# Value sums copied by ScalarE, a new order with banks given by distance, and row maxima turned by VectorE through memory, in a gated attention and GLU kernel

## The chip, the cores and the metric

The kernel runs on one core of a Trainium2 chip. The time is that of one execution on the device, in microseconds (us). A core has TensorE (PE in the profile, its weight loads PEld), VectorE (DVE), ScalarE (ACT), GpSimd (POOL) and the sync engine (SP), which issues nearly all DMAs here. PSUM, into which TensorE writes, has eight banks of 128 partitions by 512 floats.

## The reference

```python
# x: 1 x 2048 x 512, wqkv: 512 x 1536, wo: 512 x 512, w_gate, w_up: 512 x 1792, w_down: 1792 x 512
g = sigmoid((x * gate_w).sum(-1, keepdims=True))
q, k, v = split(x @ wqkv)                       # 32 heads of 16
p = softmax(q @ k.T / sqrt(16), axis=-1)        # for each head, 2048 x 2048
a = merge_heads(p @ v) @ wo
b = (sigmoid(x @ w_gate) * (x @ w_up)) @ w_down
out = g * a + (1 - g) * b
```

All of it is float32.

## The kernel before, in words

**Numbers.** TensorE multiplies operands in a rounded float32 form. For the projections each operand is split into a rounded part (names ending in h) and the rest (l), and a product is the sum of three products (hh, hl, lh).

**Prologue.** Under 95 us: x arrives transposed, in 16 pieces (`load_x`, L181), q and k of the first eight heads and all of v are computed, q and k go to memory (q_d, k_d) and come back head by head into the tiles qs and ks (`load_pair`, L218).

**Main loop.** Heads are taken in pairs, one in partitions 0 to 63 and one in 64 to 127 (b = 0, 1; "lanes"). TensorE's array is used in two halves, which run at once. A step is 128 keys by 1024 queries of a pair; a *half* is one of the two groups of 1024 queries of a pair (32 halves in all, 16 steps each). One turn of the loop is a *period*: two steps, 256 periods. A period k issues

- t0, t1 (`st_part`, L453): four score matmuls of 64 rows for each lane, t0 for step pair k, t1 for k + 1. The rows of qs hold q and, in rows 48, 49 (lane 0) and 112, 113 (lane 1), the row maximum of each query as a rounded part and a rest, against rows of -1 in ks; so the scores come out with the maximum taken off. ScalarE takes the exponential of each bank (L455) into p;
- m0, m1 (`sm_step`, L250): four matmuls for each lane, 20 steps and more ahead, of scores without maxima; VectorE reduces each bank to a maximum by query (L252). When a half has its 64 banks, a last reduce gives m, 128 queries by 16 columns (8 query tiles, 2 lanes; L256);
- d0, d1 (`dense`, L144): 12 half-array matmuls that fill the loop with other work: q and k of later heads, then gate and up. Each sum is made of products with the lower rows of the array (d0) and the upper (d1), which write one bank, dn. Where the side changes, at the word "turn" and at the period's end, an empty instruction of POOL (a token, L155) waits for the last matmul of the one side, and the first of the other waits for the token. ScalarE copies a finished sum out of dn (L306); gate and up go to memory (gu_d, L299), and are read back after the loop;
- `values(k)` (L468): 16 matmuls of p with v into one bank. The bank is copied (L475; by VectorE, in the first four periods by ScalarE), and POOL adds the copy to the half's sum (L485). The first copy of a half is the sum itself. A half's sum goes to memory (pv_d, L487).

**The maxima's way, before.** `put_max` runs right behind the values of the period that follows the last reduce: TensorE transposes m through an identity matrix into a bank (L262), ScalarE copies the 16 x 128 (L264), POOL splits it into the rounded part and the rest (L95, L96), and SP issues four DMAs, each from 8 partitions of 128 to a row of qs (L270).

**Order and banks.** The order of a period is a string of words, written by hand, STEADY; every matmul of scores or maxima has its bank behind a colon, a number among seven (st_65 to st_67 and sm_69 to sm_72 in the rows below; the eighth bank is dn). The values have bank 5, the transposed maxima bank 0. The last 8 periods, LAST, have no maxima left to compute and half as many dense halves. Engines work through their instructions in the order in which these are issued; a matmul into a bank waits until the bank has been read.

```python
STEADY = ("t0:2 d1 m0:4 d1 t0:1 d1 m0:3 d1 t0:6 d1 d1 turn m0:0 t0:2 t1:4 "
          "d0 m1:1 t1:5 d0 d0 m1:3 t1:6 d0 d0 m1:0 d0 t1:2 m1:4 m0:1")
SUMS, MAXIMA = 5, 0
LAST = "t0 d1 t0 d1 t0 d1 turn t0 t1 t1 d0 t1 d0 t1 d0"
```

In the first four periods "m0:0 m1:6" stands ahead of STEADY, which brings the maxima from a lead of 20 steps to one of 22. In 16 periods VectorE also computes a column of gate logits from x (`logits`, L439).

**Behind the loop** the denominators are inverted (L428), and the down projection and wo are computed and put together (L634, L638).

Of the kernel before, what the change touches and what calls it, by code (L numbers as in the profile page):

```python
# [24 lines left out]
P = 128  # L25
# [10 lines left out]
LEAD = 22  # L36
# [3 lines left out]
TAIL = 8  # L40
# [4 lines left out]
def gated_mix(ctx, tc, x, xT, wqkv, wo, w_gate, w_up, w_down, gate_w, ident, out):  # L45
# [26 lines left out]
    rec_d = dram.tile([P, 512], F32, name="rec_d")  # L72

# [5 lines left out]
    idt = keep.tile([P, P], F32, name="idt")  # L79
# [18 lines left out]
    def raw_weights(src, shape, name):  # L98
        raw = keep.tile(shape, F32, name=name + "r", tag="wr", bufs=2)
        sp.dma_start(raw, src)  # L100
        return raw, shape, name

    def raw_cols(src, c0, name):
        return raw_weights(src[:, c0:c0 + P].rearrange("(k p) f -> p k f", p=P), [P, KT, P], name)
# [72 lines left out]
    def load_x(c):  # L177
        raw = mid(f"x{c}")
        cols = slice(c * 512, (c + 1) * 512)
        for k in range(KT):  # L180
            sp.dma_start(raw[:, k, :], xT[k * P:(k + 1) * P, cols])  # L181
        return raw
# [40 lines left out]
    w_q = split_weights(raw_cols(wqkv, 0, "q0"), act, dve)  # L223
    xr = {0: load_x(0)}
    for b in range(2):
# [3 lines left out]
    w_k = split_weights(raw_cols(wqkv, D, "k0"), act, dve)  # L229
# [30 lines left out]
    def put_max(half, t):  # L260
        p, i = half
        pe.transpose(t[:16, :P], mrow.pop(half).rearrange("p a b -> p (a b)"), idt)  # L262
        raw = keep.tile([16, P], F32, name=f"mr{p}_{i}", tag="mr", bufs=2)
        act.activation(raw, t[:16, :P], AF.Copy)  # L264
        hl = keep.tile([16, 2, P], F32R, name=f"mhl{p}_{i}", tag="mhl", bufs=2)
        split(hl[:, 0, :], hl[:, 1, :], raw, pool, pool)
        for b in range(2):
            for a in range(2):
                r = 64 * b + 3 * DH + a
                sp.dma_start(QS[p % 2][r:r + 1, i * 1024:(i + 1) * 1024].bitcast(F32),  # L270
                             hl[8 * b:8 * b + 8, a, :].bitcast(F32))


    wd = []

    def filling():
        jobs = [("qk", c) for c in range(1, D // P)] + [("gu", f) for f in range(NF)] + [("down", 0)]

        def raws(kind, n):
            if kind == "qk":  # L280
                return [raw_cols(wqkv, n * P, f"q{n}"), raw_cols(wqkv, D + n * P, f"k{n}")]
            if kind == "gu":
                return [raw_cols(w_gate, n * P, f"g{n}"), raw_cols(w_up, n * P, f"u{n}")]
# [35 lines left out]
    for c in range(NC):  # L319
        if c + 1 < NC:  # L320
            split_x(c + 1, xr.pop(c + 1))
        if c == 0:
            wv_r = mid("wv_r")
            sp.dma_start(wv_r, wqkv[:, 2 * D:].rearrange("(k p) f -> p k f", p=P))
# [10 lines left out]
    sp.dma_start(idt, ident)  # L335
# [20 lines left out]
    for t in range(2, NS, 2):  # L356
        two = [Sum(bankv(), tokens(t + a)) for a in range(2)]
        for g in (LOW, UP):
            first_max()
            for m in range(3 * KT):  # L360
# [4 lines left out]
                if (0, 0) in mrow and g == UP:  # L365
                    put_max((0, 0), bankm())
# [332 lines left out]
```

## Time and profile before

| | |
|---|---|
| median of 3 runs | 1772.06 us (1772.02 to 1772.82) |
| span of the profiled execution (first to last instruction) | 1769.9 us |
| TensorE clock granted | 1.000 |
| main loop: first and last value matmuls start at | 94.9 and 1538.2 us |
| VectorE busy | 1565.4 us |
| ScalarE busy | 1209.9 us |

The profile is of one execution; 2.2 us of the median lie around its span. Rows of a timeline give the start, the duration, engine, line and operation, output <- input, shapes and a count; "[0.16 <-PE st L468]" says that the engine had been idle for 0.16 us and what ended that. Rows of groups give busy time and mean duration in ns, then idle time before them. A matmul that follows another without a wait has a duration of 0.39, one that had to wait about 0.50.

### The profile page before, as it was taken

The numbers are of one execution on the slowest core, as the hardware profiler recorded it, in microseconds if no ns is written. First come the engines' busy times: TensorE is split into PE (matmuls) and PEld (weight loads), VectorE is DVE, ScalarE is ACT, GpSimd is POOL, SyncE is SP. The second block draws the span as 40 slices with busy tenths as digits, with TensorE's granted clock in tenths as the row PEclk, the third lists the DMA queues.
The fourth block names the chain that finished last, engine by engine and source line by source line (L and its number), as shares of the span: only waits on it lengthen the run. The fifth ranks groups of instructions, "written<-read, shape, count | busy, mean of one in ns | idle before, by whom it ended". The sixth has DMA issues, their size and how long they took to land.

```text
span 1769.9 us, 33479 instructions
## 1 busy us (share of the span) xinstructions
PE 1756.4 (99%) x12708; PEld 1109.5 (63%) x12708; DVE 1565.4 (88%) x2503; ACT 1209.9 (68%) x2343; POOL 477.7 (27%) x435
## 2 busy tenths in 40 slices
PE   9999999999999999999999999999999999999999
PEld 7756566666555555555666666666565665588887
DVE  6989999999999999999999999999999997456543
ACT  4177777777777777777777777777777777844221
POOL 1124343432132222222222222222222222342110
PEclk9999999999999999999999999999999999999999
DMA  9312323241312131313031212112121212367762
GB/s 247 83 37 67 79 67 91 67 102 43 79 55 67 44 84 49 84 49 84 31 71 39 65 45 60 50 53 51 50 49 51 58 46 75 114 226 249 239 190 71
DMA packets 91633, 148.78 MB, mean 84 GB/s; under 512 B 10128, under 2 KB 37904, under 8 KB 88592
## 3 DMA queue, kind: packets, MB, share of 16 engines
q1 hardware_dynamic: 91472, 146.64, 29.9%
q8 instruction: 100, 1.64, 0.4%
q14 instruction: 61, 0.50, 0.1%
HBM read 87.10 MB, written 58.98 MB: 83 GB/s over the span
## 4 chain that ended last, share of the span: by engine, by line
PE 96%; DVE 3%; DMA 1%; issue 0%; ACT 0%; SPq 0%; DVEq 0%; POOL 0%
PE st L468 26%; PE dn L144 25%; PE sm L453 11%; PE sm L661 7%; PE sm L250 6%; PE st L250 5%; PE st L453 5%; PE st L131 4%; PE dn L661 2%; DVE stat L252 1%; PE st L144 1%; PE st L570 1%; PE sm L570 1%; PE sm L468 1%; DVE part L475 1%; DVE xn L439 1%
## 5 line engine op out<-in xcount | busy, mean ns | idle before, releaser
L252 DVE TENSOR_REDUCE stat<-sm 128x1 f32<-128x512 f32 x1554 | 971.5, 681 | 9.8 <-PE sm L250 6.3
L455 ACT ACTIVATE p<-sm 128x512 f32<-128x512 f32 x1029 | 608.5, 625 | 303.5 <-PE dn L144 196.6
L250 PE MATMUL sm<-ks,qs 48*128 48x512 f32 x1554 | 632.1, 415 | 0.1
L455 ACT ACTIVATE p<-st 128x512 f32<-128x512 f32 x1019 | 564.6, 635 | 14.3 <-PE st L453 10.7
L485 POOL TENSOR_TENSOR sum<-sum,part 128x512 f32<-128x512 f32 x224 | 289.3, 1292 | 868.9 <-PE sm L453 685.6
L468 PE MATMUL st<-p,v 128*17 128x512 f32 x4000 | 478.1, 595 | 0.0
L453 PE MATMUL st<-qs,ks 64*128 64x512 f32 x1019 | 422.8, 419 | 7.9 <-DVE stat L252 5.9
L453 PE MATMUL sm<-qs,ks 64*128 64x512 f32 x1029 | 425.2, 419 | 0.0
L252 DVE TENSOR_REDUCE stat<-st 128x1 f32<-128x512 f32 x494 | 336.5, 682 | 2.5 <-PE st L250 0.9
L453 PEld LDWEIGHTS sm<-qs,ks 64*128 64x128 f32 x1029 | 190.0, 186 | 209.5 <-issue 105.5
L250 PEld LDWEIGHTS sm<-ks,qs 48*128 48x128 f32 x1554 | 283.7, 184 | 29.4 <-DVE stat L252 10.1
L468 PEld LDWEIGHTS st<-p,v 128*17 128x17 f32 x4000 | 92.7, 96 | 216.9 <-issue 155.8
L453 PEld LDWEIGHTS st<-qs,ks 64*128 64x128 f32 x1019 | 188.6, 186 | 47.6 <-DVE stat L252 16.6
L250 PE MATMUL st<-ks,qs 48*128 48x512 f32 x494 | 195.0, 395 | 0.5 <-ACT p L455 0.5
L475 DVE COPY part<-st 128x512 f32<-128x512 f32 x216 | 149.3, 691 | 40.0 <-PE st L468 38.0
L250 PEld LDWEIGHTS st<-ks,qs 48*128 48x128 f32 x494 | 91.4, 185 | 21.2 <-ACT p L455 1.1
L417 DVE TENSOR_TENSOR gul<-gul 128x1024 f32<-128x1024 f32 (+1 forms) x30 | 46.1, 1542 | 35.9 <-ACT gul L416 33.7
L661 PE MATMUL sm<-wd_h,hl 128*128 128x512 f32 x208 | 68.3, 395 | 0.0
L306 ACT ACTIVATE gu<-dn 128x512 f32<-128x512 f32 x98 | 66.5, 679 | 0.0
L93 ACT ACTIVATE hl<-gul 128x1024 fp32r<-128x1024 f32 (+1 forms) x30 | 29.9, 997 | 40.1 <-PE sm L661 26.0
L96 POOL TENSOR_TENSOR ol<-ot,oh 128x1024 fp32r<-128x1024 f32 x8 | 19.3, 2412 | 113.8 <-ACT oh L93 113.8
L93 ACT ACTIVATE oh<-ot 128x1024 fp32r<-128x1024 f32 x8 | 8.5, 1061 | 57.0 <-DVE ot L619 51.7
(459 smaller groups left out, 2978.4 us busy)
## 6 DMA issues: line engine op xcount, KB each, us to landing
gu_d<-gu SPq DMA_DIRECT2D x112, 256.0 KB
gul<-gu_d SPq DMA_DIRECT2D x56, 512.0 KB
qs<-q_d SPq DMA_DIRECT2D x90, 128.0 KB
ks<-k_d SPq DMA_DIRECT2D x90, 128.0 KB
pv_d<-sum SPq DMA_DIRECT2D x32, 256.0 KB
q_d<-qe SPq DMA_DIRECT2D x12, 512.0 KB
k_d<-qe SPq DMA_DIRECT2D x12, 512.0 KB
x<-in_xT_dram SPq DMA_DIRECT2D x16, 256.0 KB
```

The lines of the kernel that those rows point to most:

```text
L131: pe.matmul(o, a, b, start=(i == 0), stop=(i == len(ops) - 1))
L144: mm = pe.matmul(self.o, a[rows], b[rows], start=(self.n == 0), stop=(self.n == 2 * len(self.ops) - 1))
L250: pe.matmul(t, qs[r:r + KM, qt * P:(qt + 1) * P], ks[r:r + KM, g * 512:(g + 1) * 512], start=True, stop=True)
L252: dve.tensor_reduce(stat[half][:, b, qt % 8, g:g + 1], t, axis=AX.X, op=ALU.max)
L306: leave = lambda e, o: act.activation(e, o, AF.Copy)
L417: dve.tensor_tensor(gu[:, 1, a], gu[:, 0, a], gu[:, 1, a], ALU.mult)
L453: pe.matmul(o, ks[r:r + KR, (kt + a) * P:(kt + a + 1) * P], qs[r:r + KR, q0:q0 + 512], start=True, stop=True)
L455: act.activation(pt[:, 2 * a + c, :], o, AF.Exp, scale=DH ** -0.5)
L468: pe.matmul(o[32 * c:32 * c + VW, :], v[:, 2 * k % 16 + a, h * VW:(h + 1) * VW], pts[c // 2][:, 2 * a + c % 2, :], start=(a == 0), stop=(a ...
L475: dve.tensor_copy(e, o)
L485: pool.tensor_tensor(s, s, e, ALU.add)
L661: pe.matmul(down[t], a, b, start=(f == 0 and m == 0), stop=(f == NF - 2 and m == 5))
```

## The change

1. ScalarE copies the value sum in every period.
2. The order of the period is a new string without banks. A bank is now taken by distance: the n-th allocation of the loop (t, m or values, 17 in a period) gets the bank that was given REUSE[n mod 17] allocations before.
3. The maxima are split by POOL in their [128, 16] form (`split_max`, right behind the values of the period whose last maxima they are). At the word "turn" of the next period VectorE transposes the 128 x 32 of rounded parts and rests by blocks of 32 x 32, SP stores the result in a new buffer m_d in memory (128 rows of 128 bytes), and four DMAs read from it into the rows of qs, each 32 pieces of 128 bytes (`turn_max`). TensorE's transpose, ScalarE's copy and the identity matrix are gone.
4. The lead is 20 steps throughout: the additional maxima matmuls of the first four periods are gone, and LAST begins ten periods before the end instead of eight, six of these with eight dense halves and four with six.
5. The host lays x, the weights of q and k, gate and up out by tiles of 128 x 128, so that a weight load reads 2 KB rows instead of 512 B; wv too is laid out as it is loaded. The first q and k weights are issued by ScalarE's queue, so that x comes first on SP's.

The core of the diff:

```diff
-    def put_max(half, t):
+    def split_max(half):
+        hl = keep.tile([P, 2, 16], F32R, name=f"mhl{half[0]}_{half[1]}", tag="mhl", bufs=2)
+        split(hl[:, 0, :], hl[:, 1, :], mrow.pop(half).rearrange("p a b -> p (a b)"), pool, pool)
+        turning.append((half, hl))
+
+    def turn_max():
+        half, hl = turning.pop(0)
         p, i = half
-        pe.transpose(t[:16, :P], mrow.pop(half).rearrange("p a b -> p (a b)"), idt)
-        raw = keep.tile([16, P], F32, name=f"mr{p}_{i}", tag="mr", bufs=2)
-        act.activation(raw, t[:16, :P], AF.Copy)
-        hl = keep.tile([16, 2, P], F32R, name=f"mhl{p}_{i}", tag="mhl", bufs=2)
-        split(hl[:, 0, :], hl[:, 1, :], raw, pool, pool)
+        mt = keep.tile([P, 32], F32, name=f"mt{p}_{i}", tag="mt", bufs=2)
+        dve.transpose(mt, hl.rearrange("p a b -> p (a b)").bitcast(F32))
+        sp.dma_start(m_d[p, i], mt)
+        rows = m_d[p, i].rearrange("(g a b t) j -> a b t g j", g=4, a=2, b=2)
         for b in range(2):
             for a in range(2):
                 r = 64 * b + 3 * DH + a
-                sp.dma_start(QS[p % 2][r:r + 1, i * 1024:(i + 1) * 1024].bitcast(F32),
-                             hl[8 * b:8 * b + 8, a, :].bitcast(F32))
+                sp.dma_start(QS[p % 2][r:r + 1, i * 1024:(i + 1) * 1024].bitcast(F32).rearrange(
+                    "o (t g j) -> o t g j", g=4, j=32), rows[a, b].unsqueeze(0))
...
         def put(e):
-            if k < LEAD - FIRST << 1:
-                act.activation(e, o, AF.Copy)
-            else:
-                dve.tensor_copy(e, o)
+            act.activation(e, o, AF.Copy)
...
+    given = [*seven, *seven]
+    count_given = [0]
+
+    def place():
+        b = given[-REUSE[count_given[0] % len(REUSE)]]
+        count_given[0] += 1
+        given.append(b)
+        return b
...
             if word == "turn":
                 turn(run)
                 work(1)
+                if turning:
+                    turn_max()
...
-    STEADY = ("t0:2 d1 m0:4 d1 t0:1 d1 m0:3 d1 t0:6 d1 d1 turn m0:0 t0:2 t1:4 "
-              "d0 m1:1 t1:5 d0 d0 m1:3 t1:6 d0 d0 m1:0 d0 t1:2 m1:4 m0:1")
+    STEADY = ("t0 m1 d1 m0 t0 d1 d1 m0 d1 t0 d1 m0 d1 turn t0 t1 m0 "
+              "d0 m1 m1 d0 d0 t1 d0 t1 t1 d0 d0 m1")
+    REUSE = (5, 8, 6, 6, 10, 7, 7, 6, 8, 7, 7, 6, 8, 6, 8, 7, 7)
+    LAST = ["t0 d1 t0 d1 t0 d1 d1 turn t0 t1 t1 d0 t1 d0 t1 d0 d0"] * (TAIL - 4) + [
+        "t0 d1 t0 d1 t0 d1 turn t0 t1 t1 d0 t1 d0 t1 d0"] * 4
...
-        if k < LEAD - FIRST << 1:
-            emit("m0:0 m1:6", **parts)
...
         values(k)
-        for half in ahead:
-            put_max(half, seven[MAXIMA])
+        for half in list(mrow):
+            split_max(half)
```

Three places show what this does to the queues. The first is TensorE's, in the middle of a period of the loop; L453 is t, L250 m, L144 d, L468 the values, and a wait for DVE or Activation ahead of t or m is that for its bank. Before, the second part of a period up to the values:

```order
L250 MATMUL sm_72<-ks_107,qs_106 128x512 [waits DVE_49]
L453 MATMUL st_67<-qs_106,ks_107 128x512 [waits Activation_49]
L144 MATMUL dn<-xh,g7h 128x512
L144 MATMUL dn<-xl,g7h 128x512
L250 MATMUL sm_69<-ks_107,qs_106 128x512 [waits DVE_49]
L144 MATMUL dn<-xh,g7l 128x512
L453 MATMUL sm_71<-qs_106,ks_107 128x512 [waits Activation_49]
L250 MATMUL st_65<-ks_107,qs_106 128x512 [waits Activation_49]
L250 MATMUL sm_70<-ks_107,qs_106 128x512 [waits DVE_49]
L468 MATMUL st_66<-p_1_11122,v 17x512 [waits Activation_49]
```

After (t is L460, d is L143, the values L475), from the word "turn" on:

```order
L460 MATMUL sm_69<-qs_106,ks_107 128x512 [waits DVE_49]
L460 MATMUL sm_70<-qs_106,ks_107 128x512 [waits Activation_49]
L250 MATMUL sm_72<-ks_107,qs_106 128x512 [waits DVE_49]
L143 MATMUL dn<-xh,g7h 128x512 [waits Pool_sequencer_49]
L250 MATMUL st_65<-ks_107,qs_106 128x512 [waits Activation_49]
L250 MATMUL sm_71<-ks_107,qs_106 128x512 [waits Activation_49]
L143 MATMUL dn<-xl,g7h 128x512
L143 MATMUL dn<-xh,g7l 128x512
L460 MATMUL st_66<-qs_106,ks_107 128x512 [waits DVE_49]
L143 MATMUL dn<-xh,g7h 128x512
L460 MATMUL sm_69<-qs_106,ks_107 128x512 [waits Activation_49]
L460 MATMUL st_67<-qs_106,ks_107 128x512 [waits DVE_49]
```

What moved: before, the last matmul of the period is one of maxima that waits for VectorE; after, the waits for VectorE stand at the matmul of maxima behind "turn" and at two of t1, and no maxima matmul but one is left behind them.

The second place is VectorE's queue around the end of a half of maxima (L256). Before:

```order
L252 TENSOR_REDUCE stat_0_5393<-st_65 128x1 [waits PE_49]
L252 TENSOR_REDUCE stat_0_5393<-sm_70 128x1 [waits PE_49]
L256 TENSOR_REDUCE m_0_5881<-stat_0_5393 128x16 [waits DVE_49]
L475 COPY part_5892<-st_66 128x512 [waits PE_49,Activation_49,Pool_49]
L252 TENSOR_REDUCE stat_1_5898<-st_65 128x1 [waits PE_49]
L252 TENSOR_REDUCE stat_1_5898<-sm_72 128x1 [waits PE_49]
L252 TENSOR_REDUCE stat_1_5898<-sm_69 128x1 [waits PE_49]
L252 TENSOR_REDUCE stat_1_5898<-sm_70 128x1 [waits PE_49]
```

After, with the transpose at "turn" (L269):

```order
L252 TENSOR_REDUCE stat_0_5439<-sm_70 128x1 [waits PE_49]
L252 TENSOR_REDUCE stat_0_5439<-st_66 128x1 [waits PE_49]
L256 TENSOR_REDUCE m_0_5923<-stat_0_5439 128x16 [waits DVE_49]
L252 TENSOR_REDUCE stat_1_5944<-st_67 128x1 [waits PE_49]
L252 TENSOR_REDUCE stat_1_5944<-st_65 128x1 [waits PE_49]
L252 TENSOR_REDUCE stat_1_5944<-sm_70 128x1 [waits PE_49]
L252 TENSOR_REDUCE stat_1_5944<-sm_69 128x1 [waits PE_49]
L269 STREAM_TRANSPOSE mt_0_5965<-mhl_0_5938 128x32 [waits DMAHW0_49,Pool_49]
L252 TENSOR_REDUCE stat_1_5944<-st_65 128x1 [waits PE_49]
```

What moved: the copy that stood ahead of a period's first reduce is gone, and the transpose of the maxima stands behind the fourth reduce of the period that follows their end.

The third place is SP's queue, the maxima of one half. Before, with the load of k's weights behind them:

```order
L270 DMA qs_106<-mhl_1_1347 1x8x128 [waits DMAHW4_49,Pool_49]
L270 DMA qs_106<-mhl_1_1347 1x8x128 [waits DMAHW5_49,Pool_49]
L270 DMA qs_106<-mhl_1_1347 1x8x128 [waits DMAHW6_49]
L270 DMA qs_106<-mhl_1_1347 1x8x128 [waits DMAHW7_49]
L209 DMA k_d<-qe_1_1463 128x2x512 [waits DMAHW0_49,Pool_49]
```

After:

```order
L270 DMA m_d<-mt_1_1353 128x32 [waits DMAHW4_49,DVE_49]
L275 DMA qs_106<-m_d 1x32x32 [waits DMAHW5_49,DMAHW4_49]
L275 DMA qs_106<-m_d 1x32x32 [waits DMAHW6_49]
L275 DMA qs_106<-m_d 1x32x32 [waits DMAHW7_49]
L275 DMA qs_106<-m_d 1x32x32 [waits DMAHW0_49]
L207 DMA k_d<-qe_1_1446 128x2x512 [waits DMAHW1_49,Pool_49]
```

What moved: the four transfers wait for POOL before; after, a store that waits for VectorE stands ahead of them, and the first of the four waits for that store (DMAHW4).

More of the change, by code (lines that the diff above doesn't have):

```diff
@@ L529, in gated_mix @@
         pass
-    bank = bankm = lambda: spot[0]
+    bank = bankm = place
     for k in range(NPER):
         n = 2 * k
-        if n + LEAD == NSTEP:
+        if n + FIRST == NSTEP:
             bank = bank7
```

60 lines of the change are left out of this document (30 added, 30 removed).

## The prediction

> **What bounds the kernel now.** I read the busy line of the page first, then the chain of work that ended last, then one steady period of the main loop in the timeline, engine by engine.
>
> ```profile
> PE 1756.4 (99%) x12708; PEld 1109.5 (63%) x12708; DVE 1565.4 (88%) x2503; ACT 1209.9 (68%) x2343; POOL 477.7 (27%) x435
> ...
> PE 96%; DVE 3%; DMA 1%; issue 0%; ACT 0%; SPq 0%; DVEq 0%; POOL 0%
> ```
>
> By these lines the kernel is TensorE's alone. But a busy TensorE need not be at its full rate, so I look inside a period. The rows are TensorE's: value matmuls, the first half-array matmuls behind them, the last row of maxima scores, and the next value matmuls.
>
> ```profile
> 1200.11 1.91 PE L468 MATMUL st<-p,v 128*17 128x512 f32 x16
> 1201.95 0.50 PE L453 MATMUL sm<-qs,ks 64*128 64x512 f32 x1
> ...
> 1202.29 0.39 PE L144 MATMUL dn<-xl,u9h 64*128 64x512 f32 x1
> 1202.52 0.39 PE L144 MATMUL dn<-xh,u9l 64*128 64x512 f32 x1
> ...
> 1205.32 0.50 PE L250 MATMUL sm<-ks,qs 48*128 48x512 f32 x1
> 1205.75 0.62 PE L468 MATMUL st<-p,v 128*17 128x512 f32 x4
> ```
>
> A period is 1205.75 - 1200.11 = 5.64 us. Halves in one lane follow each other every 0.23, and two lanes run at once. A period has 28 halves, so 14 slots. The first starts 1.84 behind the values and the values wait about 0.43 behind the last one's start: 1.84 + 13 x 0.233 + 0.43 = 5.30. So 0.34 of each period is waiting that "99% busy" doesn't show. VectorE in the same period:
>
> ```profile
> 1202.19 0.69 DVE L475 COPY part<-st 128x512 f32<-128x512 f32 x1 [0.16 <-PE st L468]
> 1202.79 0.68 DVE L252 TENSOR_REDUCE stat<-st 128x1 f32<-128x512 f32 x1
> 1203.39 3.07 DVE L252 TENSOR_REDUCE stat<-sm 128x1 f32<-128x512 f32 x5
> ```
>
> The reduces follow each other every (3.07 - 0.68) / 4 = 0.598. The fourth starts at 1203.39 + 2 x 0.598 = 1204.59 and ends at 1205.27. Its bank is the one that the last maxima matmul takes, and that starts at 1205.32. Here is the ring: values end (1202.02), copy (0.17 later), first reduce (0.60), fourth reduce's end (3 x 0.598 + 0.68), matmul (0.05), values (0.43), 1.91 of values: 5.64. **VectorE's copy plus four reduces set the period**, not its sum of work and not TensorE's.
>
> A second test of this: where VectorE gets more work ahead of the reduces, the period should grow by all of it. These are the starts of value matmuls around a gate-logit operation (L439), and the groups of VectorE.
>
> ```profile
> 471.64 1.91 PE L468 MATMUL st<-p,v 128*17 128x512 f32 x16
> 477.89 1.91 PE L468 MATMUL st<-p,v 128*17 128x512 f32 x16
> ```
> ```profile
> L475 DVE COPY part<-st 128x512 f32<-128x512 f32 x216 | 149.3, 691 | 40.0 <-PE st L468 38.0 <-PE dn L144 1.0 <-POOL qe L121 0.7
> ...
> L439 DVE CUSTOM_DVE_ANT_0 xn<-xn,gwb 128x512 f32<-128x512 f32 x16 | 10.9, 682 | 0.0
> ...
> L256 DVE TENSOR_REDUCE m<-stat 128x16 f32<-128x64 f32 x32 | 7.0, 220 | 1.1
> ```
>
> 6.25 instead of 5.64: 0.61 more, which is what a 0.68 operation takes of a pipelined engine. It isn't hidden at all.
>
> **The change, part by part.** *The copy and the order together.* ScalarE takes all value copies, so a reduce no longer stands behind one. In the new order a maxima matmul (m1) is in the first slot of the period. Its reduce starts about 0.53 after that slot's start (0.49 matmul, 0.04 to wake), the next ones at 1.13, 1.73, 2.33. I put the new PE order against these. The m0 behind "turn" reuses the bank of the second reduce, which ends at 1.81; with 0.05 to the weight load and 0.11 that a stalled half starts late (its row is 0.50 instead of 0.39) it starts at 1.97, where its slot is at 1.74: 0.23 lost. This hides the token between the halves of a dense sum. The last t1 reuses the fourth reduce's bank (ends 3.01, start 3.17) and is late by another 0.03. The rest is in time. Values start 3.73 behind the first slot: 3.73 + 1.84 = 5.57, or **0.07 less per period**. The ten last periods have an order of their own, so 246 x 0.07 = -17. Eight reduces are 4.8 of the 5.57, so VectorE then idles near 0.8 a period.
>
> *ScalarE as cover.* The cost of the copy there I take as nothing:
>
> ```profile
> 1202.48 1.09 ACT L455 ACTIVATE p<-sm 128x512 f32<-128x512 f32 x2 [1.08 <-PE sm L453]
> ...
> 1204.41 1.61 ACT L455 ACTIVATE p<-st 128x512 f32<-128x512 f32 x3
> ```
>
> ```profile
> 1000.00:1100.00 100.00, 100.00 (x784) 60.35 (x782) 97.39 (x162) 76.17 (x153) 25.80 (x24) 1.00 0.21 53
> 1508.00:1527.00 19.00, 19.00 (x150) 8.59 (x150) 7.38 (x7) 19.00 (x41) 4.71 (x5) 1.00 0.17 60
> ```
>
> Its operations follow each other every (1.61 - 0.66) / 2 = 0.475. The first of the two stretches, columns PE, weight loads, VectorE, ScalarE, POOL, has 153 of them in 100 / 5.64 = 17.7 periods: 8.6 each, with the 1.08 of idle time at the period's start, just when the values end. A copy fits in: 9.6 x 0.475 = 4.6 of 5.57. Were it not covered, its 0.48 would be in each period.
>
> *What VectorE's new room swallows.* The 16 logit operations: -0.61 each, -10. The 32 reductions L256 delay the ring today by up to 5.78 - 5.64 = 0.14 (the rows below), of which I take 0.10 for 31 halves: -3. The lead of 20 steps instead of 22 drops the eight extra maxima matmuls in the first four periods; 107.97 - 101.44 is 6.53, so 0.9 each: -3.6. These are the starts of values in the head, around a half of maxima, and at the two ends of the last periods.
>
> ```profile
> 101.44 1.91 PE L468 MATMUL st<-p,v 128*17 128x512 f32 x16
> 107.97 1.91 PE L468 MATMUL st<-p,v 128*17 128x512 f32 x16
> ...
> 1403.59 1.91 PE L468 MATMUL st<-p,v 128*17 128x512 f32 x16
> 1409.37 1.91 PE L468 MATMUL st<-p,v 128*17 128x512 f32 x16
> ...
> 1493.61 1.91 PE L468 MATMUL sm<-p,v 128*17 128x512 f32 x16
> ...
> 1527.42 1.99 PE L468 MATMUL sm<-p,v 128*17 128x512 f32 x16
> 1531.35 1.05 PE L468 MATMUL st<-p,v 128*17 128x512 f32 x8
> ```
>
> *The tail.* Its periods last up to 1531.35 - 1527.42 = 3.93, and the second stretch above shows ScalarE busy in all of it: eight exponentials of 0.475 make 3.8. A ninth operation makes it 4.3. Nine such periods, 38.7, replace the two longer and seven short ones between 1493.61 and 1531.35, 37.7; the dense halves in them are as many. So +1.
>
> *Layout and loads.* Weights in the loop are loaded long ahead, nothing waits for them: 0. At the front q0's load no longer stands ahead of x:
>
> ```profile
> 0.74 0.44 SPq L100 DMA_DIRECT2D q0r<-in_wqkv_dram  x1
> ...
> 3.83 0.63 ACT L93 ACTIVATE q0h<-q0r 128x512 fp32r<-128x512 f32 x1 [1.60 <-DMA q0r<-in_wqkv_dram]
> ```
>
> x is issued 0.5 sooner (one issue); at most the 1.60 of that wait goes. I take -1.
>
> These add up to -17 - 10 - 3 - 3.6 + 1 - 1 = **-34**.
>
> *The maxima's way.* Before, all is done right behind the values: PE transpose, ScalarE copy, two POOL operations, and four transfers on SP's queue.
>
> ```profile
> 1406.44 2.75 SPq L270 DMA_DIRECT2D qs<-mhl  x4
> ```
> ```profile
> L270 SPq DMA_DIRECT2D qs<-mhl x128: 634/635/1518, 78.1 to 1498.6; - x128
> ```
> ```profile
> L299 SPq DMA_DIRECT2D gu_d<-gu x112: 314/326/936, 376.9 to 1566.9; - x112
> ```
> ```profile
> PE st L453 <- DMA qs<-mhl: 0.4, 1, 0.4
> ```
>
> They are issued 0.81 into the period, 0.70 apart, and TensorE waited for one of them once in the run. Now the path is: POOL's split early in the same period; VectorE's transpose only at "turn", behind the fourth reduce; a store to memory; its landing; then four reads, which SP can issue only after it. On the clock of that period: transpose at 2.93 (fifth reduce's place), 0.2 long (no row; 0.22 is the row of L256, and it can't be under 0), store issued at 3.17. The store's landing has no row in the views. It can't be under the 0.32 of an issue; this pair, a store and the wait that it ended, gives the upper end, 1633.14 - 1629.53 = 3.61, with 128 KB behind other transfers.
>
> ```profile
> 1629.53 0.66 SPq L429 DMA_DIRECT2D rec_d<-den  x1
> ```
> ```profile
> 1633.14 1.06 ACT L93 ACTIVATE oh<-ot 128x1024 fp32r<-128x1024 f32 x1 [5.25 <-DMA rec_d<-den]
> ```
>
> I take 1.65, near the 4 KB transfers of L270, which by the trace's landing events land 1.77 behind the start of a 0.63 issue. Reads start at 4.87; each costs SP 0.32 to 0.66, I take L270's row, 0.70 apart, since they too write one row of qs from many pieces. The fourth starts at 6.97, lands at 8.74, and its matmul can start at 8.90. That period is 5.64 long (the transpose delays the fifth reduce, for which the values wait, by 0.07), so this is 3.26 in the next. There the first t1 (slot 7, due at 1.74) uses the rows: it, and everything behind it on TensorE, stands until then. Six more slots and 0.32 (the 0.43 less the 0.11 of a stalled half's start) give values at 3.26 + 1.40 + 0.32 = 4.98 instead of 3.73. **A stall of 1.25 + 0.07 = 1.32 for each of 31 halves (the first lies ahead of the loop): +41.** ScalarE and VectorE then wait for TensorE, so nothing covers it.
>
> Sum: -34 + 41 = +7 on the profiled span of 1769.9; the median of 1772.06 is 2.2 above that span, which I leave: **1779**.
>
> The Trainium skill, "DMA: Bandwidth & Descriptors", section "Anatomy of one DMA — SWDGE (gpsimd) path", speaks against this change: it gives each transfer (fitted for GpSimd's queue) a fixed 2.0 us, most of it the receipt of the write, with device memory as the heaviest target. An estimate by that page puts 2.0 for 1.65 and for 1.77, so 0.6 more per half and a time near 1797. The landing of 1.77 for the 4 KB rows is a little under its figure, and no row here shows a small store to memory.
>
> **Rivals.** *A, faster: the chain is short enough.* The one number that decides is the stall per half; it breaks even at 34 / 31 = 1.09. If SP issues the reads as fast as L299's 0.32 to 0.4, the fourth starts 1.0 sooner and the stall is about 0.35: 1772 - 34 + 11 = 1749; with the store also landing 0.4 sooner nothing is left and it is 1738. For it: most DMA rows of SP are of this length. Against it: L270 itself, and rec_d<-den with 0.66, both of few partitions. Chance 0.25.
>
> *B, slower: the period stays 5.64.* The bank distances were fitted by hand above; if ScalarE's copy, in order ahead of an exponential, frees one bank 0.07 later than the ring allows, nothing is gained in the steady periods: -34 becomes -17, 1796. For it: only 0.6 of ScalarE's idle time is left. Against: the copy falls into the 1.08. Chance 0.12.
>
> *C, slower: each hop through memory is longer.* 0.3 more in the store and in the last read (still far below the 3.61) is 0.6 per half: 1797. Chance 0.10.
>
> **How the numbers follow.** The forecast, a faster period with a stall of 1.0 to 1.7 per half, has 0.53 and by itself 1768 to 1791. The predicted time is its 1779. The range reaches into A to 1755 and over B and C to 1804; below it lies about half of A (0.12), above it 0.05. A difference under 0.2% (3.5 us) can't be told from none. Faster: A's 0.24 and 0.04 of the forecast's low end, 0.28. Same: 0.12 of the forecast and 0.01 of A, 0.13. Slower: 0.37 of the forecast, B and C, 0.59.
>
> **What would show it.** Right: values every 5.57 in periods without maxima; the first reduce behind no copy; one period per half longer by about 1.3, with TensorE's weight load of the first t1 idle on a transfer qs<-m_d; logit periods like the others. Wrong: no such wait (A); intervals of 5.6 or more without maxima and ScalarE without idle time (B); reads issued 0.7 apart but starting later than 1.7 behind the store (C). Most of all I would be wrong if the store and the four reads together take under 4.7 instead of 5.6.

## The result, and the profile after

| | before | changed |
|---|---|---|
| median | 1772.14 us (4 runs, 1772.02 to 1772.82) | 1814.53 us (4 runs, 1813.24 to 1817.0) |
| span of the profiled execution | 1769.9 | 1813.0 |
| granted clock, mean | 1.000 | 0.991 |

The ratio is 1.0242, 95% interval 1.0227 to 1.0256: 42 us slower, where 7 were forecast and the range ended at 1804. Of the four runs of the kernel with the doubled store (below), one was in a slow state of the chip (2078 us at a granted clock of 0.782); its time is left out there, and it is the one whose profile was kept.

The busy line and the chain of work that ended last, in the page of the changed kernel:

```profile
PE 1753.0 (97%) x12676; PEld 1046.7 (58%) x12676; DVE 1417.8 (78%) x2282; ACT 1341.6 (74%) x2564; POOL 467.6 (26%) x435
...
PE 84%; DMA 6%; DVE 5%; SPq 3%; issue 1%; ACT 0%; POOL 0%; POOLq 0%
```

TensorE was 96% of that chain and is 84%. DMA and SP's queue, 1% together before, are 9% of it. The starts of the value matmuls around the maxima of one half show where that is:

```profile
1016.20 1.91 PE L475 MATMUL sm<-p,v 128*17 128x512 f32 x16
1021.81 1.91 PE L475 MATMUL sm<-p,v 128*17 128x512 f32 x16
1027.45 1.91 PE L475 MATMUL st<-p,v 128*17 128x512 f32 x16
1034.29 1.91 PE L475 MATMUL st<-p,v 128*17 128x512 f32 x16
1039.91 1.91 PE L475 MATMUL sm<-p,v 128*17 128x512 f32 x16
```

Periods without maxima last 5.61 (5.64 before), the one in which the transpose stands among the reduces 5.64, the next 6.84. These are VectorE's row of that transpose, SP's rows behind it, and the row of TensorE that waited longest:

```profile
1026.63 0.20 DVE L269 STREAM_TRANSPOSE mt<-mhl 128x32 f32<-128x32 f32 x1
```
```profile
1026.86 0.32 SPq L270 DMA_DIRECT2D m_d<-mt  x1
1027.29 0.36 SPq L216 DMA_DIRECT2D qs<-q_d  x1
1028.27 2.78 SPq L275 DMA_DIRECT2D qs<-m_d  x4
```
```profile
1032.48 0.46 PE L460 MATMUL sm<-qs,ks 64*128 64x512 f32 x1 [1.28 <-DMA qs<-m_d]
```

The store is issued 0.23 behind the transpose's start, the first read 1.41 behind the store, the four reads 0.71 apart, and the matmul starts 5.85 behind the transpose's start. The wait is 1.23 by the periods' length. That is the stall that was forecast. But it isn't always so small. Here is a half of the early loop, with the same views:

```profile
127.82 0.36 SPq L207 DMA_DIRECT2D q_d<-qe  x1
129.30 0.33 SPq L270 DMA_DIRECT2D m_d<-mt  x1
132.94 2.78 SPq L275 DMA_DIRECT2D qs<-m_d  x4
```
```profile
137.07 0.76 PE L460 MATMUL sm<-qs,ks 64*128 64x512 f32 x1 [3.42 <-DMA qs<-m_d]
```
```profile
129.90 1.91 PE L475 MATMUL st<-p,v 128*17 128x512 f32 x16
140.36 3.16 PE L475 MATMUL st<-p,v 128*17 128x512 f32 x16
147.21 1.91 PE L475 MATMUL sm<-p,v 128*17 128x512 f32 x16
```

A store of 512 KB (q_d) was issued 1.5 ahead, and the small store was followed by the first read, which waits for its landing, after 3.6 instead of 1.4. The period is 10.46 long, and the one behind it 6.85 without any wait for a transfer: the matmul's duration of 0.76 and the values' 3.16 for 1.91 say why. TensorE's clock was halved. The stretches of the clock, with busy time of TensorE, weight loads, VectorE, ScalarE and POOL, then the granted clock:

```profile
132.69:136.11 3.42, 0.97 (x10) 0.48 (x6) 2.11 (x4) 1.80 (x4) 1.26 (x1) 1.00 0.03 4
136.11:142.93 6.82, 5.86 (x30) 2.83 (x30) 2.58 (x4) 2.66 (x5) 1.50 (x2) 0.50 0.00 1
279.47:282.88 3.41, 1.32 (x12) 0.78 (x8) 2.46 (x4) 2.15 (x5) 1.26 (x1) 1.00 0.03 5
282.88:289.71 6.83, 6.41 (x30) 2.83 (x30) 2.58 (x4) 2.66 (x5) 1.88 (x2) 0.50 0.35 58
...
378.45:381.87 3.42, 1.73 (x14) 1.08 (x13) 2.48 (x4) 2.56 (x5) 1.26 (x1) 1.00 0.05 8
381.87:385.28 3.41, 2.58 (x22) 1.66 (x26) 2.04 (x4) 1.91 (x4) 0.00 (x0) 1.00 0.66 117
```

A window of 3.41 us in which TensorE was busy for 0.97 or 1.32 is followed by one or two windows at 0.50; one with 1.73 is not. Six waits of the loop are followed by half clock. The sum of the difference, by the starts of values in both traces (before, changed, in us):

| part | forecast | measured |
|---|---|---|
| steady periods | -17 | -6 (0.026 for 242) |
| logit periods | -10 | -10 |
| maxima reductions and the few odd periods | -3 | -4 |
| first periods (three of the four lie between two values) | -3.6 | -2.8 |
| last periods (the last half's wait among them) | +1 | +3 |
| up to the first values | -1 | +1.3 |
| waits for maxima: the usual 1.25 in 30 halves (the forecast counts 31 of 1.32) | +41 | +37.6 |
| waits for maxima: what is over 1.25 | 0 | +24 |
| sum | +7 | +43 (spans) |

### The profile page after: what moved, and what is told of

It reads as the page before. It is cut to its first block, busy times and chain, and to the rows that moved or that the text cites. A ratio compares the mean times of both kernels' runs of the same rounds, so it can differ in the third digit from the quotient of the medians.

```text
span 1813.0 us, 33225 instructions
## 1 busy us (share of the span) xinstructions
PE 1753.0 (97%) x12676; PEld 1046.7 (58%) x12676; DVE 1417.8 (78%) x2282; ACT 1341.6 (74%) x2564; POOL 467.6 (26%) x435
## 4 chain that ended last, share of the span: by engine, by line
PE 84%; DMA 6%; DVE 5%; SPq 3%; issue 1%; ACT 0%; POOL 0%; POOLq 0%
PE dn L143 14%; PE sm L475 13%; PE sm L460 11%; PE st L475 10%; PE sm L250 8%; PE st L460 8%; PE sm L670 7%; DVE stat L252 5%; PE st L250 4%; PE st L130 4%; SPq L275 3%; DMA qs<-m_d 3%; DMA m_d<-mt 3%; PE dn L670 2%; PE st L143 1%; PE sm L579 1%
## 5 line engine op out<-in xcount | busy, mean ns | idle before, releaser
L252 DVE TENSOR_REDUCE stat<-sm 128x1 f32<-128x512 f32 x1188 | 766.3, 681 | 110.0 <-PE sm L250 85.5
L462 ACT ACTIVATE p<-sm 128x512 f32<-128x512 f32 x1190 | 675.4, 622 | 35.9 <-PE st L250 26.5
L252 DVE TENSOR_REDUCE stat<-st 128x1 f32<-128x512 f32 x860 | 567.4, 680 | 119.7 <-PE st L250 101.4
L460 PE MATMUL sm<-qs,ks 64*128 64x512 f32 x1190 | 476.2, 424 | 35.1 <-DMA qs<-m_d 34.3
L250 PE MATMUL sm<-ks,qs 48*128 48x512 f32 x1188 | 475.1, 435 | 0.2
L250 PE MATMUL st<-ks,qs 48*128 48x512 f32 x860 | 364.4, 445 | 0.0
L460 PE MATMUL st<-qs,ks 64*128 64x512 f32 x858 | 342.7, 419 | 19.9 <-DMA qs<-m_d 18.0
L460 PEld LDWEIGHTS sm<-qs,ks 64*128 64x128 f32 x1190 | 221.0, 186 | 215.8 <-ACT p L462 97.0
L475 PE MATMUL sm<-p,v 128*17 128x512 f32 x2096 | 250.7, 595 | 0.0
L250 PEld LDWEIGHTS sm<-ks,qs 48*128 48x128 f32 x1188 | 214.1, 186 | 51.3 <-DVE stat L252 31.8
L475 PE MATMUL st<-p,v 128*17 128x512 f32 x2000 | 242.4, 602 | 0.0
L460 PEld LDWEIGHTS st<-qs,ks 64*128 64x128 f32 x858 | 159.0, 186 | 120.6 <-ACT p L462 49.8
L250 PEld LDWEIGHTS st<-ks,qs 48*128 48x128 f32 x860 | 155.2, 186 | 29.7 <-DVE stat L252 20.5
L479 ACT ACTIVATE part<-st 128x512 f32<-128x512 f32 x124 | 75.2, 607 | 103.8 <-issue 88.6
L475 PEld LDWEIGHTS sm<-p,v 128*17 128x17 f32 x2096 | 48.8, 97 | 122.9 <-issue 81.5
L475 PEld LDWEIGHTS st<-p,v 128*17 128x17 f32 x2000 | 46.6, 97 | 122.0 <-issue 84.4
```

Source lines behind the costliest of these rows:

```text
L250: pe.matmul(t, qs[r:r + KM, qt * P:(qt + 1) * P], ks[r:r + KM, g * 512:(g + 1) * 512], start=True, stop=True)
L252: dve.tensor_reduce(stat[half][:, b, qt % 8, g:g + 1], t, axis=AX.X, op=ALU.max)
L460: pe.matmul(o, ks[r:r + KR, (kt + a) * P:(kt + a + 1) * P], qs[r:r + KR, q0:q0 + 512], start=True, stop=True)
L462: act.activation(pt[:, 2 * a + c, :], o, AF.Exp, scale=DH ** -0.5)
L475: pe.matmul(o[32 * c:32 * c + VW, :], v[:, 2 * k % 16 + a, h * VW:(h + 1) * VW], pts[c // 2][:, 2 * a + c % 2, :], start=(a == 0), stop=(a ...
L479: act.activation(e, o, AF.Copy)
```

## Experiments

The theory is that TensorE's wait for the maxima's rows costs all of the loss, through the chain's usual lateness, late stores and the clock; the rivals are that the new order, the copies or the transfers themselves cost it.

**The order of the reads.** Lane 1's rows are needed first (t1), and are read last.

```diff
-        for b in range(2):
+        for b in (1, 0):
```

> The changed kernel (1814.5 us) with the four reads of a half's maxima issued in another order: the two for lane 1 first, which the first t1 waits for, then the two for lane 0, which are needed a period later. Theory (TensorE stands in 30 periods for the last of the four reads, 1.25 us in the usual half, and in six of them so long that the granted clock falls): lane 1's rows land 2 x 0.70 us sooner, the usual stall goes, what is left is the part by which the store landed late in the early halves (12 us in all), clock drops gone: 1814.5 - 37.5 - 11 = 1766, between 1760 and 1772. Rival (the new order with its bank distances costs the time, the waits for the reads only stand where another wait would stand anyway): within 5 us of 1814.5.

Measured: 1763.62 (1763.35 to 1763.83), ratio to before 0.9956, interval 0.9940 to 0.9973. One word in the program takes back 51 us and brings the changed kernel 8 us under the kernel before. The usual half has no wait left; the rows of the waits view are now

```profile
PE sm L460 <- DMA qs<-m_d: 5.7, 5, 1.9
PE st L460 <- DMA qs<-m_d: 3.3, 4, 1.3
```

against these of the changed kernel:

```profile
PE sm L460 <- DMA qs<-m_d: 34.3, 20, 3.4
```
```profile
PE st L460 <- DMA qs<-m_d: 18.0, 11, 2.8
```

So order, copies and layout are not what costs; the wait for these rows is.

**Transpose right behind the split.**

```diff
             split_max(half)
+            turn_max()
```

> The changed kernel with VectorE's transpose, the store and the reads issued right behind POOL's split, at the end of the period in which the last maximum is found, instead of at the word turn of the next period. Theory (only the lateness of the chain costs): it starts about 3 us sooner, which covers the usual lateness of 1.25 and the latest stores (2.2 more): all stalls in the loop go, 1814.5 - 61.5 = 1753, between 1748 and 1760. Rival (the hops through memory are themselves what costs, by contention with other transfers or by VectorE's added work): no lower than 1780.

Measured: 1775.04 (1773.07 to 1777.04), 22 over what the theory gave, under the 1780 of the rival, and 39 under the changed kernel. TensorE's waits for the rows fell from 52.3 us in 31 to 3.7 in 5, and a new wait came: VectorE stands at the transpose until POOL has split the maxima, and all reduces queue behind it. Waits view of this kernel:

```profile
DVE mt L269 <- POOL mhl L95: 28.0, 32, 2.1
```

In the usual half this makes a period 5.82 instead of 5.61; in the first six, where POOL has q and k to split first (1.9 us), 7.3 and more. The chain can be early without costing only where its input is ready.

**Work inside the wait.** Five matmuls of no use ahead of the first t1 in each period that waits; nothing of the computation changes.

```diff
+            if word == "t1" and fill_now:
+                fill_now.pop()
+                o = given[-REUSE[count_given[0] % len(REUSE)]]
+                for _ in range(5):
+                    pe.matmul(o, z.to_broadcast([P, P]), z.to_broadcast([P, 512]), start=True, stop=True)
...
+        fill_now[:] = [1] if k % 8 == 7 and k < NPER - TAIL else []
```

> The changed kernel with five matmuls of no use (128 x 512, into the bank that the next t1 overwrites) ahead of the first t1 in each period that waits for maxima, about 1.1 us of work inside the stall. Theory (an idle TensorE of some 2.9 us or more has its clock halved for 3.4 or 6.8 us, which costs 11 us over six halves of the changed kernel): the idle time stays under 2.8 in all halves, the granted clock is 1.00 in the loop and the time falls by about 11 to 1803 although work is added. Rival (the half clock falls in time that is waiting anyway, and costs nothing): 1814 or a little more, since five matmuls are added.

Measured: 1809.62 (1809.23 to 1809.91): 5 faster than the changed kernel by doing 150 matmuls more. The half-clock stretches in the loop fell from six to two, and the size was half of what I expected. All six places of the changed kernel are free of it. The two that are left (375 and 1120 us) lie behind stores that landed later in this run than in that of the changed kernel (3.7 instead of 2.6, 3.3 instead of 1.5), while the one at 746.8 (741.0 here) landed in time. So some of the 5 can be the stores' and not the clock's.

**The copies alone**, in the kernel before:

```diff
-            if k < LEAD - FIRST << 1:
-                act.activation(e, o, AF.Copy)
-            else:
-                dve.tensor_copy(e, o)
+            act.activation(e, o, AF.Copy)
```

> The kernel before (1772.1 us) with one thing changed: ScalarE copies the value sums in all periods; order, banks, lead, the maxima's way and the layout are those of before. Theory (VectorE's copy ahead of four reduces is the ring that sets the period of 5.64): the first reduce starts when the second-slot maxima matmul ends, 0.07 sooner, 17 us in all, and the logits and the reduction of maxima disappear in VectorE's idle time, 10 and 3: 1742, between 1735 and 1755. Rival (a copy in ScalarE's queue delays exponentials, and with them banks and values, by as much): within 5 us of 1772, or slower.

Measured: 1760.89 (1760.25 to 1763.53), ratio 0.9943: between the range of the theory and that of the rival. The logits' 10 us went, the period did not: 5.63 in place of 5.57. Nor did the 3 for the reduction of maxima: the period with it still lasts 5.79. Values and their weight load in this kernel:

```profile
1197.50 1.91 PE L468 MATMUL st<-p,v 128*17 128x512 f32 x16
1203.13 1.91 PE L468 MATMUL st<-p,v 128*17 128x512 f32 x16
```
```profile
1202.64 0.18 PEld L250 LDWEIGHTS st<-ks,qs 48*128 48x128 f32 x1 [0.23 <-ACT p L455]
1202.64 0.18 PEld L250 LDWEIGHTS sm<-ks,qs 48*128 48x128 f32 x1
1203.13 0.13 PEld L468 LDWEIGHTS st<-p,v 128*17 128x17 f32 x8 [0.30 <-ACT p L455]
```

TensorE now waits for an exponential, ahead of which the copy stands in ScalarE's queue, both for the last bank of maxima and for that of the values. In the median period the first reduce starts 0.07 sooner, as worked out, and the fourth ends 0.06 sooner; the period is only 0.015 shorter, so about 0.05 of it is given back between the fourth reduce and the values, where these waits for ScalarE stand.

**The old way under the new order.** PE transpose, ScalarE copy and transfers within the core, right behind the values, into the bank that the next t0 takes.

```diff
         for half in list(mrow):
-            split_max(half)
+            put_max(half, given[-REUSE[count_given[0] % len(REUSE)]])
...
```

> The changed kernel with the maxima put as before (PE transpose, ScalarE copy, POOL split, four DMAs within the core), right behind the values of the period in which the last maximum is found; order, bank distances, lead of 20, copies by ScalarE and layout stay as changed. Theory (the way through memory is what costs, order and lead are good for about 18 us together): no wait for the rows, about 0.1 more per half for the transpose and the copy, 1753 + 3 = 1756, between 1750 and 1762. Rival (a lead of 20 steps is too short for any way): the stalls stay, over 1785.

Measured: 1785.61 (1785.33 to 1786.4), what the rival gave, though not by its reason: no wait for the rows is left, but the bank was badly chosen. The transpose, the copy and the t0 stand one behind the other:

```profile
1047.53 0.27 PE L263 MATMUL sm<-idt,m 128*16 128x128 f32 x1 [0.16 <-DVE m L257]
1047.98 0.25 ACT L265 ACTIVATE mr<-sm 16x128 f32<-16x128 f32 x1
...
1048.28 0.50 PE L455 MATMUL sm<-qs,ks 64*128 64x512 f32 x1 [0.48 <-ACT mr L265]
```

That is 1.0 to 1.25 us per half of another kind (periods of 6.60 and 6.86). The time doesn't tell the theories apart; that the rows come in time at a lead of 20 steps speaks against the rival.

**A lead of 22 steps again**, everything else as changed but the last periods, of which there are eleven, with an order of their own:

```diff
-TAIL = FIRST // 2
+LEAD = 22
+TAIL = LEAD // 2
...
+        if k < LEAD - FIRST << 1:
+            bankm = lambda: given[-5]
+            emit("m0", **parts)
+            bankm = lambda: given[-6]
+            emit("m1", **parts)
+            bankm = place
...
```

> The changed kernel with a lead of 22 steps again: one more m0 and m1 in each of the first four periods, eleven last periods instead of ten; the way through memory stays. Theory (the chain misses its use by 1.25 to 3.5 us, the steps ahead decide): the maxima of a half are complete 5.6 us sooner, every stall in the loop goes; the head costs 3 or 4 more, the granted clock is 1.00 in the loop: 1814.5 - 61.5 + 4 = 1757, between 1751 and 1764. Rival (hops through memory cost by contention): over 1785.

Measured: 1756.18 (1755.66 to 1756.75), ratio 0.9908, interval 0.9893 to 0.9923: the fastest kernel of the study. No wait of TensorE for qs<-m_d is left, and the chain of a usual half is as long as in the changed kernel:

```profile
1027.38 0.32 SPq L271 DMA_DIRECT2D m_d<-mt  x1
1028.83 2.75 SPq L276 DMA_DIRECT2D qs<-m_d  x4
```

Late stores are still there: two (667.6 and 1252.3 us) landed only after 3.4 and 3.2, and TensorE didn't wait. It is not the hops but the time left for them that decides. In the first six halves there is also less to hide: the small store is now issued 4 us ahead of q_d's and not 1.5 behind it, and lands in 1.4 to 2.2.

**The store on ScalarE's queue.**

```diff
-        sp.dma_start(m_d[p, i], mt)
+        act.dma_start(m_d[p, i], mt)
```

> The changed kernel with one thing moved: the store of the turned maxima is issued on ScalarE's queue, the four reads stay on SP's. Theory (in eight halves the store landed 1 to 2.2 us late because it stood behind 512 KB and 256 KB stores in SP's queue): these halves come down to the usual 1.25, clock drops with them: 1814.5 - 12 - 11 = 1791, between 1786 and 1798. Rival (the transfers of both queues share the same engines, so the store is as late there; or ScalarE's issue costs more than it brings): within 4 us of 1814.5 or above.

Measured: 1814.42 (1812.18 to 1817.07): the rival. By the landing events of the trace the store of the same early half took 3.4 on this queue, about as late as on SP's (3.6), and those of the next five 2.3 to 2.7 (2.4 to 2.7 on SP's): another queue is no way around the large store. And the issue stands in ScalarE's queue until VectorE's transpose is done (0.23 behind its start, as on SP), with exponentials behind it:

```profile
1026.13 0.33 ACTq L270 DMA_DIRECT2D m_d<-mt  x1
1026.50 1.09 ACT L462 ACTIVATE p<-st 128x512 f32<-128x512 f32 x2 [1.33 <-PE dn L143]
```

That makes the period with the transpose 6.98 long in nearly every half (5.64 on SP's queue), and the one behind it shorter, 5.6 or some 6.3 in most (6.84 on SP's). The loss has moved; that the sum comes out as in the changed kernel is chance.

**Both: lane 1 first, and the chain behind the third reduce.**

```diff
-        for b in range(2):
+        for b in (1, 0):
...
+            elif word == "max":
+                if turning:
+                    turn_max()
...
-    STEADY = ("t0 m1 d1 m0 t0 d1 d1 m0 d1 t0 d1 m0 d1 turn t0 t1 m0 "
+    STEADY = ("t0 m1 d1 m0 t0 d1 d1 m0 max d1 t0 d1 m0 d1 turn t0 t1 m0 "
...
```

> The changed kernel with the reads for lane 1 first and with transpose, store and reads issued behind the second m0 of the period instead of at turn (VectorE's transpose then stands behind three reduces instead of four). Theory: the chain ends 1.4 + 0.6 us sooner for the first user; only a store that lands over 0.7 late can still be waited for (six early halves, two later ones, 0.3 to 1.4 each, 5 us in all), without a clock drop: 1753 + 5 = 1758, between 1752 and 1763. Rival (VectorE then waits for POOL's split, as it does when the transpose is issued right behind the split): 1768 or more.

Measured: 1762.35 (1761.77 to 1764.09), 4 over the expectation and inside its range. The early halves still wait, and the transpose now stands ahead of the reduce whose bank a t1 takes, 0.10 per half (1030.75 to 1036.46 between values, 5.71).

**What the clock costs.** The store issued twice, one behind the other (a longer chain, the same result), and the same with ten matmuls of no use inside the wait (the edit of the five above, with ten).

```diff
         sp.dma_start(m_d[p, i], mt)
+        sp.dma_start(m_d[p, i], mt)
```

> The changed kernel with the store of the turned maxima issued twice, one behind the other, so that the chain is one hop of about 1.45 us longer in each of 31 halves, and no other work is added. Theory of the clock (a window of 3.41 us in which TensorE is idle for some 1.9 us or more is followed by one at half clock, at about 1.9 us each): the idle time per half grows from 1.7 to 3.1, so four halves in five get a half-clock window: 1814.5 + 45 for the hops + 36 for the clock = 1895, and the granted clock is about 0.975. Rival (the half clock costs nothing beyond the wait): 1814.5 + 45 = 1860.

> The kernel with the store issued twice, and ten matmuls of no use (about 2.2 us) inside each wait for the maxima, so that TensorE is idle for 0.9 instead of 3.1 us per half. Theory of the clock: no half-clock windows but one or two, and the time is that of the hops alone, 1814.5 - 11 + 45 = 1848, some 45 below the same kernel without the added matmuls. Rival (the half clock costs nothing): equal to the kernel without the added matmuls, or longer.

Measured: 1921.73 (1913.45 to 1921.91) without, 1862.0 (1861.19 to 1868.86) with the added matmuls; the mean granted clock is 0.957 to 0.962 without and 0.993 to 0.996 with them. 300 matmuls more make the kernel 60 us faster. The chain is the same in both, so the half clock that the idle waits bring costs about 60 / 31 = 1.9 us more per half. That it costs time is shown, and more than the 36 that I had put; how late the stores landed without the added matmuls is not known. The kernel with the added matmuls is 14 over the 1848 that I expected for the chain alone: three half-clock stretches are left in its loop, and in 14 halves its second store landed 0.4 to 1.9 later than the usual 1.42, 12 us in all. What makes these late isn't shown.

**The additional maxima matmuls one per period**, on the kernel with the lead of 22:

```diff
-        if k < LEAD - FIRST << 1:
...
+        if k < LEAD - FIRST << 2:
+            bankm = lambda: given[-6]
+            emit(("m0", "m1")[k % 2], **parts)
```

> The kernel with the new order, the way through memory and a lead of 22 steps (1756.2 us), with the eight additional maxima matmuls one per period over eight periods instead of two per period over four. Theory (two per period make ten reduces of 0.6, over what VectorE does in a period, one per period makes nine, 5.4, which fits): the first periods cost 0.25 more each for eight of them instead of 1.27 for four: 1753, between 1751 and 1756, the fastest of all. Rival (the additional matmul waits for its bank wherever it stands): 1756 to 1762.

Measured: 1759.73 (1756.56 to 1760.88): no gain. The first periods last 6.2, which is 0.6 more than a steady one and not 0.25. In the profiled run (1760.88) one early half waits again for its rows (2.2 us), since the lead grows more slowly, and 6.83 us at half clock follow.

**The new way alone**, in the kernel before, with its lead of 22 (the edit is that of the change, part 3):

```diff
-        for half in ahead:
-            put_max(half, seven[MAXIMA])
+        for half in list(mrow):
+            split_max(half)
...
```

> The kernel before (1772.1 us) with the maxima's new way alone: POOL's split, VectorE's transpose at turn of the next period, store and four reads; order, banks, lead of 22 steps, VectorE's copies and layout as before. Theory (the way through memory takes 5.7 us or more, but costs only where less than that is left before the first use): with two more steps nothing waits; the PE transpose goes (0.1 per half), VectorE's transpose of 0.2 stands in a full VectorE (0.14 per half): 1772, between 1768 and 1777, granted clock 1.00. Rival (the way itself costs): over 1785.

Measured: 1768.78 (1767.06 to 1769.89), ratio 0.9976, interval 0.9967 to 0.9986: 4 us faster than the kernel before in the same series (1772.96). With the copies' 11 that makes 15 of the 16 by which the kernel with the lead of 22 is under before. If the parts add up, the new order with its bank distances and the layout, which come on top there, are worth about 1 together; no run has either of them alone.

## Why the prediction was wrong

**The bound now.** That VectorE's work ahead of the reduces isn't hidden held: the logit periods gave their 10 back in both kernels with ScalarE's copies. That a busy TensorE hides 0.34 of waiting in each period is worked out from rows; of this wait the change took back 0.026.

**The steady period failed by size.** 0.07 was worked out, 0.026 came. The rows of a period in the changed kernel, TensorE's first and last ones and VectorE's reduces:

```profile
1203.38 0.49 PE L460 MATMUL sm<-qs,ks 64*128 64x512 f32 x1
1203.39 0.49 PE L250 MATMUL st<-ks,qs 48*128 48x512 f32 x1
...
1206.52 0.46 PE L460 MATMUL sm<-qs,ks 64*128 64x512 f32 x1
...
1206.83 0.39 PE L143 MATMUL dn<-xh,g8l 64*128 64x512 f32 x1
1207.15 0.62 PE L475 MATMUL sm<-p,v 128*17 128x512 f32 x4
```
```profile
1203.95 0.69 DVE L252 TENSOR_REDUCE stat<-st 128x1 f32<-128x512 f32 x1 [0.73 <-PE st L250]
1204.56 2.47 DVE L252 TENSOR_REDUCE stat<-sm 128x1 f32<-128x512 f32 x4
```

The first reduce starts 0.57 behind the slot, not 0.53; the fourth ends at 3.05, not 3.01. The last t1 (its duration of 0.46 says that it waited) starts 0.09 behind that, the values 0.63 behind the t1, 3.77 behind the slot instead of 3.73. The ring is the one that I named, and the 0.044 that are missing count 242 times: 11 us. The waits view names VectorE for the values as well, whose own bank is that of the fifth reduce; but this ends 0.12 ahead of them, and where the transpose delays it by 0.12 the period grows by 0.03 only.

**The usual stall held**, in part by luck. 1.25 measured, 1.32 forecast. Transpose 0.20 as taken; the store landed in 1.40, not 1.65; the reads were 0.71 apart, taken as 0.70 (their issue has 0.65), and the last one landed in about 1.95, not 1.77. The errors of the two landings, 0.25 and 0.18, have opposite signs and nearly cancel. The Trainium skill, "DMA: Bandwidth & Descriptors", "Anatomy of one DMA — SWDGE (gpsimd) path", has a fixed 2.0 for each, fitted for GpSimd's queue. On SP's queue here the reads agree (1028.27 + 2.78 - 0.65 to 1032.48 is 2.1 with TensorE's start), the store to memory is 0.6 under it. Rival C had no part in the usual half.

**What failed is the step that took this stall as the same in all halves, with nothing behind it.** I counted 31 times one number, taken from an idle queue, and put what lies over it at nothing, without a reason; it measured 24 of the 36 us between 1779 and 1814.5 (11 more are the steady period's). Eight of the halves had a store that landed 1.0 to 2.2 later: 11 or 12 us by the landing events. Six of them are the first six, behind a 512 KB store 1.5 us ahead; I had quoted a hop of 3.61 as the upper end and put 0.10 on it, and it came here (3.6), where it had a reason that the profile of before showed (q_d and k_d are stored there). The other two (746.8 and 1351.1 us) have no such store: a 256 KB one was issued 3.5 us ahead, as in the 22 later halves that landed in 1.4 to 1.6. What the two have, and the latest of the six too, is a transfer of 16 KB of the kind that the DMA view calls "instruction" within the 1.4 us behind the issue of the store. Two late stores of the kernel with the lead of 22 (667.6 and 1252.3) have one too. That this is their cause was not tested.

**And the clock.** The clock of before is 1.00 up to the last microsecond, and its one wait for a row of maxima is 0.4 long. I let the clock stand at 1.00 under a wait that I had worked out to be over a microsecond on top of the matmul's own pipeline. What is left of the 24 us, about 12, I put down to half clock behind six waits; the pair with the doubled store gives 1.9 us per half, which fits. The six waits had 2.9 to 3.8 between the starts of two matmuls (TensorE idle for 2.5 to 3.4), and a window with TensorE busy for 1.32 of 3.41 was enough. The Trainium skill, "TensorE: Matmul & The Clock Gate", in its section "HAM oscillation — how this bites in real kernels", speaks of idle gaps over about 3.4 us. Here the clock fell sooner than that. It isn't the length of a wait alone, either: the one that ended at 382.70 was as long as another (idle for 2.5) and no half clock followed; it lay across two windows (the last two rows of the clock above).

**Front and end.** The first values came 1.3 later, not 1 sooner: a half-clock stretch lies there too (0.84 in the mean from 85 to 95 us, 1.00 before). The kernel before with the new way alone has one as well (0.85), and so has the changed kernel with the old way (0.77); the kernel with the copies alone has none. No run tested its cause. The end has periods of 4.27 with ScalarE's ninth operation, as worked out, but the first two of them last 5.10 and 5.44, the second with the last half's wait: +3.

**Rivals.** A (the chain hidden) was not what came, but it is what the smallest edit makes of the kernel: 1763.6 with two reads exchanged, inside the range for A. B's condition, an exponential late behind the copy, came true in the kernel with the copies alone, and cost there about 0.05 a period. In the changed kernel its first sign came as well, intervals of 5.6 and more (5.61), but not the second: ScalarE is idle for 1.0 in each period. C's condition, reads later than 1.7 behind the store, was met in the eight late halves, where it cost more than C's 0.6.

## What to carry to other kernels

A chain that misses its use by a microsecond is cheapest mended by what the first user needs first: the order of four reads was worth 51 us here, and two steps of lead 58. Work out a new wait for the busiest stretch and not only for the quiet one, and ask what TensorE's clock does behind it. An instruction put early on an engine is no gain if its input is late, since the whole queue stands with it.

## What the runs showed of the hardware

- The clock goes by windows of 3.41 us on a grid that is fixed within a run: the half-clock stretches at 136.11, 282.88 and 753.92 us start whole multiples of 3.413 apart. In the changed kernel every window with TensorE idle for 1.9 us or more was followed by one or two at half clock, none with 1.7 or less. In other kernels of the study single windows with 1.2 (early transpose) or 1.4 us (store on ScalarE's queue) of idle time were followed by half clock too, so where the limit lies, and what counts as idle when only half of the array works, stays open.
- A 16 KB store of 128 rows of 128 bytes to memory lands in 1.40 us beside nothing, in 2.3 to 3.6 behind a 512 KB store issued 1.5 us ahead, on the same queue or on another.
- A DMA that gathers 32 pieces of 128 bytes into one row occupies SP for 0.65 us, one of 128 rows for 0.32, though it moves 4 KB and not 16:

```profile
L275 SPq DMA_DIRECT2D qs<-m_d x128: 649/650/814, 79.7 to 1541.2; - x128
```
```profile
L270 SPq DMA_DIRECT2D m_d<-mt x32: 319/320/499, 77.6 to 1536.5; - x32
```
- A block transpose of 128 x 32 on VectorE takes 0.20 us and delays the next reduce by 0.12.
